# Attention decode with a gated feed-forward layer on one core: the first keys go ahead of the weights into the values' buffer, keys and values share one tensor, and the last values come in six loads instead of nine

## The chip, the core and the metric

The kernel runs on one core of a Trainium2 chip. The metric is the device time of one execution in microseconds, the median of several runs. A smaller time is better. The profile comes from one execution recorded by the hardware profiler.

## The reference

Two sequences (B = 2) of one token each go through one transformer block. All numbers are float32.

```
x: [2, 1, 448]; k_cache, v_cache: [2, 16, 8192, 256]; wq: [448, 4096]; wo: [4096, 448]
q      = layernorm(x) @ wq                     # 16 heads of 256, for each of 2 sequences
scores = q . k_cache * 256**-0.5               # 8192 keys a head
o      = softmax(scores) . v_cache
h      = x + o @ wo
g, u   = layernorm(h) @ w_gate, layernorm(h) @ w_up      # 448 -> 1792
out    = h + (g * u) @ w_down                  # 1792 -> 448
```

There are 32 pairs of a head and a sequence. The text calls each a query and numbers them 0 to 31. Each query has its own 8192 keys and 8192 values, 8.39 MB of either. Together with the weights this is 561 MB that have to come from the chip's memory.

## The kernel before

**Slots.** The 8192 keys of a query lie on 128 partitions, 64 keys on each. One key of all partitions is called a slot here: 256 floats on each of 128 partitions. "64 keys" or "32 values" in this document means so many slots. The buffer for keys, `k_sb`, has 112 slots (L245), the buffer for values, `v_sb`, has 64 (L246). Query i's keys go to the slots 0 to 63 for an even i and 48 to 111 for an odd i (L276). The 16 slots 48 to 63 thus belong to both, and the kernel works them off first (L446): for an even query they hold its last 16 keys, for an odd one its first 16.

**Work on a query.** VectorE multiplies the keys in place with the query (L462) and sums over the 256 numbers (L468), in two parts of 16 and 48 keys; the last two queries have four parts of 16 (L447). It then finds the maximum. TensorE and ScalarE make the softmax of it, and TensorE multiplies the weights of the softmax with the values (`mix`, L496). While VectorE works on query n, the values of query n-1 come in and are mixed. TensorE runs the mixes of the queries before `LOOP` in a hardware loop and the later ones in straight code.

**Loads.** Nearly all loads are issued by SyncE, on one queue, in the order of the program (L612 to L634): for each n the first part of the values of n-1, then the keys of n+1, then any further parts of the values of n-1, and every eighth query a block of weights. A helper (L146 to L176) finds out which earlier instructions still use the slots that a load writes, and puts waits for them ahead of the load. A waiting load holds up all loads behind it on SyncE. A wait for TensorE goes to the next of its matmuls that raises a semaphore; in a mix that is the last matmul of each part (L509).

**Query 0.** Its keys come in two loads, the last 24 of them and the first 40 (`FIRST`, L22), both behind the first block of weights (L303). The product of the 24 keys is written to the values' buffer (L459), so that the slots 48 to 63 are free for query 1's keys as soon as the multiply is over. The values of query 0 wait for that buffer.

**The end.** The values of the last four queries come in parts with places of their own (`LATE`, L25): 48 + 16 slots for query 28, 32 + 32 for 29, 32 + 32 for 30 (the second in the keys' buffer), 16 + 32 + 16 for 31. Behind them come the weights of the feed-forward layer (gate, up, down) into the keys' buffer (L660 to L670). After query 31's keys TensorE mixes its values, but ahead of the last part it starts the sums for the residual (`open_sums`, L598), then come the output projection of the last head, the gate and up projections, and the down projection, whose weights are the last to land.

Of the kernel before, what the change touches and what calls it, by code (L numbers as in the profile page):

```python
# [7 lines left out]
ALU = mybir.AluOpType  # L8
# [10 lines left out]
OVER = HC  # L19

AHEAD = 24
FIRST = ((NJ - AHEAD, NJ), (0, NJ - AHEAD))  # L22


LATE = (  # L25
    ((48, None), (16, None)),
    ((32, None), (32, None)),
    ((32, None), (32, ("k", 0))),
    ((16, ("k", 32)), (32, ("v", 32)), (16, ("v", 0))),
)  # L30
WQ, WO = 3 * 2 * DH + DH, 2 * D
WALL = 2 * WQ + 4 * WO
# [183 lines left out]
def decode_block(nc, x, k_cache, v_cache, w, wg, wu, wd, out):  # L216
# [3 lines left out]
    def sb(name, *shape):  # L220
        return nc.alloc_sbuf_tensor(name, list(shape), F32)[:]
# [20 lines left out]
        put("PE", "transpose", out, in_, ident[:n, :n], r=(*r, "ident"), w=w, mark=mark)  # L242

    sb("align", P, ALIGN)
    k_sb = sb("k_sb", P, 2 * NJ - OVER, DH)  # L245
    v_sb = sb("v_sb", P, NJ, DH)  # L246
    w_sb = sb("w_sb", P, WALL)
    buffers = {"k": k_sb, "v": v_sb}
    v_flat = v_sb.rearrange("p j d -> p (j d)")

    def guest(name, at, rows, *shape):

        n = 1
        for k in shape:
            n *= k
        o.homes[name] = ("v", at, n)
        got = v_flat[:rows, at : at + n]
        if len(shape) > 1:
            dims = "abc"[: len(shape)]
            got = got.rearrange(f"p ({' '.join(dims)}) -> p {' '.join(dims)}", **dict(zip(dims, shape)))  # L260
        return got
# [5 lines left out]
        h, b = divmod(i, B)  # L267
        return cache[b, h].rearrange("(p j) d -> p j d", p=P)[:, lo:hi, :]

    def load_keys(name, cache, i, lo, hi, buf, at, event=None):  # L270
        o.load(
            "SP", name, buffers[buf][:, at : at + hi - lo, :], keys(cache, i, lo, hi),
            writes=[(buf, at * DH, (at + hi - lo) * DH)], event=event,
        )

    def k_base(i):  # L276
        return i % 2 * (NJ - OVER)

    def load_k(i, lo=0, hi=NJ):
        load_keys(f"d_k_{i}_{lo}", k_cache, i, lo, hi, "k", k_base(i) + lo)  # L280

    def v_parts(i):
        got, lo = [], 0
        for n, place in LATE[i - EARLY] if i >= EARLY else ((NJ, None),):
            buf, at = place or ("v", lo)
            got.append((lo, lo + n, buf, at))
            lo += n
        return got

    def load_v(i, part):  # L290
        lo, hi, buf, at = part
        load_keys(f"d_v_{i}_{lo}", v_cache, i, lo, hi, buf, at, "e_v" if i < LOOP else None)

    def load_w(name, k, lo, hi, event=None):
        o.load("SP", name, w_sb[:, lo:hi], w[k][:, lo:hi], writes=[("w", lo, hi)], event=event)
# [4 lines left out]
    def wo_at(h):  # L300
        return 2 * WQ + h % 4 * WO

    load_w("d_w0", 0, 0, WQ)  # L303
    for lo, hi in FIRST:
        load_k(0, lo, hi)

    ident = sb("ident", P, P)
    put("POOL", "memset", ident, 0.0, w=["ident"])
# [134 lines left out]
    def score_parts(i):  # L443
        if i == 0:
            return list(FIRST)
        at = [(k - 1) % (NJ // HC) * HC if i % 2 == 0 else k * HC for k in range(NJ // HC)]  # L446
        if i in FINE:  # L447
            return [(lo, lo + HC) for lo in at]
        return [(at[0], at[0] + HC), (at[1], at[1] + NJ - HC)]

    def scores(i, part, between=None):
        h, b = divmod(i, B)
        s, name = s_t[i % 2], f"s{i % 2}"
        lo, hi = score_parts(i)[part]
        at = k_base(i) + lo
        kt = k_sb[:, at : at + hi - lo, :]
        qk, there = kt, ("k", at * DH, (at + hi - lo) * DH)
        if i == 0 and part == 0:
            qk, there = v_sb[:, : hi - lo, :], ("v", 0, (hi - lo) * DH)  # L459
        q, slot = qs[b], q_at(h)  # L460
        here = ("k", at * DH, (at + hi - lo) * DH)
        dve(  # L462
            "tensor_mul", qk, kt, q[:, slot, :][:, None, :].to_broadcast([P, hi - lo, DH]),
            r=[here, (f"q{b}", slot, slot + 1)], w=[there],
        )
        if between is not None:
            between()
        dve("tensor_reduce", s[:, lo:hi], qk, axis=AX.X, op=ALU.add, r=[there], w=[(name, lo, hi)])  # L468

    def top(i):  # L470
        dve("tensor_reduce", m, s_t[i % 2], axis=AX.X, op=ALU.max, r=[f"s{i % 2}"], w=["m"],
# [24 lines left out]
    def mix(i, parts):  # L496
        k = other(i)
        with common(i):
            take("e_v", i, 16)
            for lo, hi, buf, at in parts:  # L500
                for t in range(lo // 2, hi // 2):
                    g, j = 32 * (t % 4), at + 2 * t - lo
                    mm(
                        o_ps[k][g : g + 2, :], p_t[k][:, 2 * t : 2 * t + 2],
                        buffers[buf][:, j : j + 2, :], t < 4, t >= NJ // 2 - 4,
                        r=[f"p{k}", (buf, j * DH, (j + 2) * DH)], w=[f"o_ps{k}"],
                        mark="PE" if t == hi // 2 - 1 else None,
                    )

# [71 lines left out]
    def group(t, q):  # L581
        return t[:, q * YW : (q + 1) * YW]

    late_at = [HC * DH]

    def late_guest(name, rows, *shape):
        got = guest(name, late_at[0], rows, *shape)
        late_at[0] += o.homes[name][2]
        assert late_at[0] <= 2 * HC * DH
        return got  # L590

    h_sb = late_guest("h_sb", B, DC * P)
# [19 lines left out]
    for n in range(NQ + 1):  # L612
        hp, at = divmod(n, 2 * B)
        parts = v_parts(n - 1) if n > 0 else []
        if n > 0:
            load_v(n - 1, parts[0])
        if n < NQ:
            scores(n, 0, (lambda: softmax(n - 1)) if n > 0 else None)
        else:
            softmax(n - 1)  # L620
        if late is not None:
            mix(n - 2, late)
            mixed(n - 2)
            late = None
        if n + 1 < NQ:
            load_k(n + 1)
        for part in parts[1:]:
            load_v(n - 1, part)
        if n % 8 == 1:
            k = n // 8 + 1  # L630
            load_w(f"d_w_{k}", k, WQ if k == H // 4 else 0, WALL, event("e_w", n))
        def norm_last():
            if n > 0:
                norm(n - 1)  # L634

        if n == NQ:
            norm_last()
        else:
            for part in range(1, len(score_parts(n))):
                scores(n, part, norm_last if part == 1 else None)  # L640
        if n == NQ:
            mix(n - 1, parts[:-1])
            open_sums()
            mix(n - 1, parts[-1:])
            mixed(n - 1)
        elif n + 1 < NQ and len(parts) > 1:
            late = parts[1:]
            mix(n - 1, parts[:1])
        elif n > 0:
            mix(n - 1, parts)  # L650
            mixed(n - 1)
        if at == 2 and hp + 1 < H // 2:
            queries(n - 1, hp + 1)
        if n < NQ:
            if n == 0:
                o.ops["PE"].append(lambda: turns())
            top(n)

    k_flat = k_sb.rearrange("p j d -> p (j d)")
    places = {"wd": 0, "wg": (NJ - OVER) * DH, "wu": (NJ - OVER) * DH + NF * D}  # L660
    wd_t, wg_t, wu_t = (k_flat[:, places[n] :][:, : NF * D] for n in ("wd", "wg", "wu"))
    for name, t, src in (("wg", wg_t, wg), ("wu", wu_t, wu)):
        for k, half in enumerate(PIECES[name]):
            o.load("SP", f"d_{name}_{k}", t[:, half], src[:, half],
                   writes=[("k", places[name] + half.start, places[name] + half.stop)])
    at = 0
    for n in DOWN:
        o.load("SP", f"d_wd_{at}", wd_t[:, at * D : (at + n) * D], wd[:, at * D : (at + n) * D],
               writes=[("k", at * D, (at + n) * D)])
        at += n  # L670

    o.load(
# [6 lines left out]

    def project(out, out_name, t, name, k, between=None):  # L680
        wide, piece = WIDE[{"wg": "B_w_gate", "wu": "B_w_up"}[name]][k], PIECES[name][k]
        here = ("k", places[name] + piece.start, places[name] + piece.stop)
        t = t[:, piece]
        for c in range(DC):
            for g in range(4):
                xs = xr[:, c]
                if c < DC - 1:
                    at = c * sum(wide) + sum(wide[:g])
                else:
                    xs = xr[:, c + g % 2]  # L690
                    at = 3 * sum(wide) + (wide[0] if g >= 2 else 0)
                mm(
                    out[32 * g : 32 * g + 32, : wide[g]], xs.rearrange("p b r -> p (b r)"),
                    t[:, at : at + wide[g]], c == 0, c == DC - 1, r=["xr", here], w=[out_name],
                    mark="PE" if c == DC - 1 and g == 3 else None,
                )
            if c == 1 and between is not None:
                between()
# [54 lines left out]
    def down(lo, hi):  # L753
        for k in range(lo, hi):
            n, g = FF[k]
            for q in range(YN):
                mm(
                    y_ps[32 * q : 32 * q + 32, :], hmT[n // 2][:, n % 2, g, :],
                    wd_t[:, k * D + q * YW : k * D + (q + 1) * YW], False, k == NF - 1,
                    r=[f"hmT{n // 2}", ("k", k * D, (k + 1) * D)], w=["y_ps"],  # L760
                    mark="PE" if k == NF - 1 and q == YN - 1 else None,
                )

# [94 lines left out]
```

## Time and profile before

| | |
|---|---|
| median of 3 runs | 1301.37 us (1301.36 to 1301.38) |
| profiled execution, its span | 1300.5 us |
| rest of the median around the span | 0.9 us |
| VectorE busy | 1130.8 us (87%) |
| TensorE busy (matmul) | 488.8 us (38%) |
| ScalarE busy | 62.6 us (5%) |
| bytes moved, mean rate | 561.45 MB, 432 GB/s |

The span runs from the first to the last instruction of the profiled execution. Busy times are those of instructions that compute. Loads are issued by SyncE and carried out by 16 DMA engines. In the profile VectorE is DVE, TensorE is PE, ScalarE is ACT and SyncE is SP (its queue of issues SPq). Nearly all instructions have the line of a helper, L229 or L176, so that they are told apart by the tiles they write and read: `k_sb<-k_sb,q` is the multiply with the query, `s<-k_sb` the sum, `o_ps<-v_sb,p` the mix.

### The profile page before, as it was taken

The numbers are of one execution on the slowest core, as the hardware profiler recorded it, in microseconds if no ns is written. First come the engines' busy times: TensorE is split into PE (matmuls) and PEld (weight loads), VectorE is DVE, ScalarE is ACT, GpSimd is POOL, SyncE is SP. The second block draws the span as 40 slices with busy tenths as digits, with TensorE's granted clock in tenths as the row PEclk, the third lists the DMA queues.
The fourth block names the chain that finished last, engine by engine and source line by source line (L and its number), as shares of the span: only waits on it lengthen the run. The fifth ranks groups of instructions, "written<-read, shape, count | busy, mean of one in ns | idle before, by whom it ended". The sixth has DMA issues, their size and how long they took to land.

```text
span 1300.5 us, 6955 instructions
## 1 busy us (share of the span) xinstructions
PE 488.8 (38%) x2972; PEld 168.9 (13%) x2972; DVE 1130.8 (87%) x275; ACT 62.6 (5%) x184; POOL 1.4 (0%) x9
## 2 busy tenths in 40 slices
PE   3035422363331633215343063432424334243368
PEld 2011100120100201002101021010111001010113
DVE  7996988888988689888889868898888897889991
ACT  1000000000000000000000000000000000000000
POOL 0000000000000000000000000000000000000000
PEclk8566756686656766558666576665766667666578
DMA  9999999999999999999999999999999999999998
GB/s 414 423 434 448 424 437 431 427 441 423 448 424 435 448 423 443 427 439 429 435 435 423 433 448 423 448 424 443 427 443 427 423 436 445 426 438 429 435 433 374
DMA packets 12111, 561.45 MB, mean 432 GB/s; under 512 B 1602, under 2 KB 1732, under 8 KB 1988
## 3 DMA queue, kind: packets, MB, share of 16 engines
q1 hardware_dynamic: 12096, 561.30, 99.8%
q8 instruction: 6, 0.10, 0.0%
q14 instruction: 5, 0.04, 0.0%
q10 hardware_dynamic: 4, 0.00, 0.0%
HBM read 561.19 MB, written 0.11 MB: 432 GB/s over the span
## 4 chain that ended last, share of the span: by engine, by line
DMA 70%; DVE 29%; PE 0%; issue 0%; SPq 0%
DMA k_sb<-in_A_k_cache_dram 68%; DVE k_sb L229 14%; DVE s L229 14%; DMA k_sb<-in_wd_dram 2%; DVE nm L229 0%; PE y_ps L229 0%; SPq L176 0%; DVE m L229 0%; PE sm L229 0%; DVE v_sb L229 0%; DVE rl L229 0%
## 5 line engine op out<-in xcount | busy, mean ns | idle before, releaser
L229 DVE TENSOR_TENSOR k_sb<-k_sb,q 128x12288 f32<-128x12288 f32 (+2 forms) x67 | 549.6, 8203 | 130.3 <-DMA k_sb<-in_A_k_cache_dram 130.3
L229 DVE TENSOR_REDUCE s<-k_sb 128x48 f32<-128x12288 f32 (+2 forms) x67 | 549.3, 8198 | 0.2
L229 PE MATMUL o_ps<-v_sb,p 128*2 128x512 f32 x2000 | 288.2, 739 | 397.7 <-PEq L183 387.6
L229 PEld LDWEIGHTS o_ps<-v_sb,p 128*2 128x2 f32 x2000 | 53.7, 97 | 603.8 <-issue 591.3
L229 PE MATMUL sm<-nm,ones 1*128 1x1 f32 x64 | 16.6, 326 | 191.7 <-PEq L183 175.1
L229 PE MATMUL sm<-ident,m 128*1 128x128 f32 x32 | 10.9, 341 | 137.0 <-PEq L183 106.1
L229 PE MATMUL q_ps<-w_sb,xb 128*128 128x256 f32 (+1 forms) x172 | 59.3, 503 | 0.0
L229 ACT ACTIVATE o_sb<-o_ps 128x512 f32<-128x512 f32 x32 | 19.1, 597 | 703.9 <-PE o_ps L229 703.9
L229 PE MATMUL sm<-sel,o_sb 128*128 128x1 f32 x256 | 33.7, 253 | 25.8 <-PEq L183 22.9
L229 PE MATMUL acc_ps<-w_sb,oT 128*2 128x448 f32 x60 | 36.6, 749 | 15.9 <-PEq L183 11.0
L229 PEld LDWEIGHTS sm<-nm,ones 1*128 1x128 f32 x64 | 14.6, 283 | 201.2 <-issue 183.5
L229 PEld LDWEIGHTS sm<-sel,o_sb 128*128 128x128 f32 x256 | 31.8, 195 | 55.6 <-issue 48.2
L229 PEld LDWEIGHTS q_ps<-w_sb,xb 128*128 128x128 f32 x172 | 33.7, 200 | 30.0 <-issue 27.6
L229 PE MATMUL sm<-lsum,ones 128*128 128x1 f32 x64 | 17.5, 342 | 26.0 <-PEq L183 23.1
L229 ACT ACTIVATE nb<-sm 128x1 f32<-128x1 f32 x32 | 5.5, 171 | 395.7 <-PE sm L229 395.7
L229 PEld LDWEIGHTS sm<-ident,m 128*1 128x1 f32 x32 | 2.6, 81 | 149.8 <-issue 115.3
L229 PEld LDWEIGHTS sm<-lsum,ones 128*128 128x128 f32 x64 | 15.6, 303 | 28.0 <-issue 24.7
L229 ACT ACTIVATE q<-q_ps,rstd 128x512 f32<-128x512 f32 (+1 forms) x18 | 11.5, 640 | 71.9 <-PE q_ps L229 71.9
L229 PE MATMUL o_ps<-k_sb,p 128*2 128x512 f32 x48 | 9.3, 934 | 6.1 <-DMA k_sb<-in_A_v_cache_dram 6.1
L229 ACT ACTIVATE p<-s,nb 128x64 f32<-128x64 f32 x32 | 11.1, 347 | 1.0
L229 DVE TENSOR_TENSOR v_sb<-k_sb,q 128x6144 f32<-128x6144 f32 x1 | 6.6, 6557 | 4.8 <-DMA k_sb<-in_A_k_cache_dram 4.8
L229 PE MATMUL q_ps<-k_sb,xr 128*32 128x256 f32 (+3 forms) x96 | 10.0, 506 | 1.6 <-DMA k_sb<-in_B_w_gate_dram 1.6
(79 smaller groups left out, 85.1 us busy)
## 6 DMA issues: line engine op xcount, KB each, us to landing
v_sb<-in_A_v_cache_dram SPq DMA_DIRECT2D x4, 4096.0 KB, 30.5
w_sb<-in_w_dram SPq DMA_DIRECT2D x3, 3584.0 KB, 37.8
v_sb<-in_A_v_cache_dram SPq DMA_DIRECT2D x1, 6144.0 KB, 24.3
k_sb<-in_A_k_cache_dram SPq DMA_DIRECT2D x1, 5120.0 KB, 24.6
v_sb<-in_A_v_cache_dram SPq DMA_DIRECT2D x2, 2048.0 KB, 27.3
k_sb<-in_A_v_cache_dram SPq DMA_DIRECT2D x1, 4096.0 KB, 35.3
k_sb<-in_B_w_gate_dram SPq DMA_DIRECT2D x1, 3136.0 KB, 32.4
k_sb<-in_A_k_cache_dram SPq DMA_DIRECT2D x1, 3072.0 KB, 11.6
```

Source lines behind the costliest of these rows:

```text
L229: o.put(engine, lambda: f(*args, **kw), r, w, mark, event)
```

## The change

Keys and values share one tensor `c_sb` of 112 + 64 slots, whose last 64 (from `RING` on) are the values' buffer. Even queries now have the upper 64 of the 112 slots for keys and odd ones the lower 64. The 16 shared slots are still the first to be worked off: an even query's first 16 keys and an odd query's last 16.

Query 0's first 24 keys are loaded ahead of the weights, to the values' buffer, and multiplied in place there. Its other 40 keys follow behind the weights, to slots 72 to 111. Query 1's keys go to the slots 0 to 63, which nothing uses before.

The values of query 28 come in one load like those before it, so that TensorE's loop has 29 turns. Query 29 has 32 + 32 values, query 30 all 64 in one load to the slots 64 to 127 of the joint tensor, query 31 46 + 18, the 18 in slots 64 to 81. The weights of the feed-forward layer have other places in the slots, and the sums for the residual start ahead of the whole mix of query 31.

```diff
-FIRST = ((NJ - AHEAD, NJ), (0, NJ - AHEAD))
+FIRST = ((0, AHEAD), (AHEAD, NJ))
+RING = 2 * NJ - OVER
 LATE = (
-    ((48, None), (16, None)),
-    ((32, None), (32, None)),
-    ((32, None), (32, ("k", 0))),
-    ((16, ("k", 32)), (32, ("v", 32)), (16, ("v", 0))),
+    ((32, RING), (32, RING + 32)),
+    ((64, NJ),),
+    ((46, RING + 16), (18, NJ)),
 )
...
-    k_sb = sb("k_sb", P, 2 * NJ - OVER, DH)
-    v_sb = sb("v_sb", P, NJ, DH)
+    c_sb = sb("c_sb", P, RING + NJ, DH)
+    v_sb = c_sb[:, RING:, :]
...
     def k_base(i):
-        return i % 2 * (NJ - OVER)
+        return (1 - i % 2) * (NJ - OVER)
...
+    load_keys("d_k_first", k_cache, 0, *FIRST[0], RING)
     load_w("d_w0", 0, 0, WQ)
-    for lo, hi in FIRST:
-        load_k(0, lo, hi)
+    load_k(0, *FIRST[1])
...
-        at = [(k - 1) % (NJ // HC) * HC if i % 2 == 0 else k * HC for k in range(NJ // HC)]
+        at = [(k - i % 2) % (NJ // HC) * HC for k in range(NJ // HC)]
...
-        at = k_base(i) + lo
-        kt = k_sb[:, at : at + hi - lo, :]
-        qk, there = kt, ("k", at * DH, (at + hi - lo) * DH)
-        if i == 0 and part == 0:
-            qk, there = v_sb[:, : hi - lo, :], ("v", 0, (hi - lo) * DH)
+        at = RING if i == 0 and part == 0 else k_base(i) + lo
+        kt, here = c_sb[:, at : at + hi - lo, :], rows(at, hi - lo)
...
-    late_at = [HC * DH]
+    late_at = [0]
...
         if n == NQ:
-            mix(n - 1, parts[:-1])
             open_sums()
-            mix(n - 1, parts[-1:])
+            mix(n - 1, parts)
             mixed(n - 1)
...
-    places = {"wd": 0, "wg": (NJ - OVER) * DH, "wu": (NJ - OVER) * DH + NF * D}
+    places = {"wg": 0, "wu": NF * D, "wd": (NJ + 20) * DH}
```

## Rows read from the trace of the kernel before

**Rows 1.** The page: span, busy time of each engine, and the loads' queue.

```profile
span 1300.5 us, 6955 instructions
...
PE 488.8 (38%) x2972; PEld 168.9 (13%) x2972; DVE 1130.8 (87%) x275; ACT 62.6 (5%) x184; POOL 1.4 (0%) x9
...
q1 hardware_dynamic: 12096, 561.30, 99.8%
```

**Rows 2.** Windows: one query. Columns: busy PE, PEld, DVE, ACT, POOL; clock; DMA share; GB/s.

```profile
1120.77:1159.40 38.63, 14.69 (x81) 4.17 (x81) 35.01 (x7) 1.47 (x5) 0.00 (x0) 0.63 1.00 431
```

**Rows 3.** Chain of waits, queries 29 and 30: start us, length us, what.

```profile
1129.76 29.64 DMA k_sb<-in_A_k_cache_dram
...
1159.42 4.43 DVE k_sb L229
...
1164.03 4.33 DVE s L229
...
1194.47 4.33 DVE k_sb L229
...
1225.25 4.43 DVE s L229
```

**Rows 4.** Timeline of SyncE's issues, same stretch: start us, length us, what.

```profile
1168.39 0.33 SPq L176 DMA_DIRECT2D k_sb<-in_A_k_cache_dram  x1
1168.76 13.36 SPq L176 DMA_DIRECT2D v_sb<-in_A_v_cache_dram  x2
1203.34 0.33 SPq L176 DMA_DIRECT2D k_sb<-in_A_k_cache_dram  x1
```

**Rows 5.** Timeline of VectorE, query 0's first multiply; in brackets the idle time before.

```profile
12.83 6.56 DVE L229 TENSOR_TENSOR v_sb<-k_sb,q 128x6144 f32<-128x6144 f32 x1 [4.83 <-DMA k_sb<-in_A_k_cache_dram]
```

**Rows 6.** Timeline of TensorE, the first queries' matmuls.

```profile
7.30 9.25 PE L229 MATMUL q_ps<-w_sb,xb 128*128 128x256 f32 x32
```

**Rows 7.** Timeline of ScalarE, the first query scaled.

```profile
11.10 0.47 ACT L229 ACTIVATE q<-q_ps,rstd 128x256 f32<-128x256 f32 x1 [1.85 <-PE q_ps L229]
```

**Rows 8.** Chain of waits, query 2's keys from issue to landing.

```profile
57.05 27.09 DMA k_sb<-in_A_k_cache_dram
```

**Rows 9.** Timeline of TensorE, the first mix.

```profile
64.97 9.31 PE L229 MATMUL o_ps<-v_sb,p 128*2 128x512 f32 x64 [10.20 <-PEq L183]
```

**Rows 10.** DMA issues into an empty queue: count, KB, us from issue to landing.

```profile
w_sb<-in_w_dram SPq DMA_DIRECT2D x1, 896.0 KB, 4.8
...
out_dram<-v_sb SPq DMA_DIRECT2D x1, 56.0 KB, 1.6
```

**Rows 11.** Timeline of TensorE, mixes and matmuls that wait for loads at the end.

```profile
1207.80 6.20 PE L229 MATMUL o_ps<-v_sb,p 128*2 128x512 f32 x32 [0.75 <-DMA v_sb<-in_A_v_cache_dram]
...
1236.92 5.30 PE L229 MATMUL o_ps<-v_sb,p 128*2 128x512 f32 x32 [0.53 <-DMA v_sb<-in_A_v_cache_dram]
...
1256.26 5.87 PE L229 MATMUL o_ps<-k_sb,p 128*2 128x512 f32 x32 [6.05 <-DMA k_sb<-in_A_v_cache_dram]
...
1275.63 1.90 PE L229 MATMUL o_ps<-v_sb,p 128*2 128x512 f32 x16 [0.27 <-DMA v_sb<-in_A_v_cache_dram]
...
1283.13 3.63 PE L229 MATMUL q_ps<-k_sb,xr 128*32 128x512 f32 x16 [1.60 <-DMA k_sb<-in_B_w_gate_dram]
...
1296.47 2.03 PE L229 MATMUL y_ps<-k_sb,v_sb 128*32 128x112 f32 x64 [0.71 <-DMA k_sb<-in_wd_dram]
```

**Rows 12.** Timeline of TensorE, two whole mixes and one of 16 values.

```profile
1101.58 9.83 PE L229 MATMUL o_ps<-v_sb,p 128*2 128x512 f32 x64 [12.74 <-PEq L183]
...
1140.22 9.29 PE L229 MATMUL o_ps<-v_sb,p 128*2 128x512 f32 x64 [12.73 <-PEq L183]
...
1200.87 3.59 PE L229 MATMUL o_ps<-v_sb,p 128*2 128x512 f32 x16
```

**Rows 13.** Timeline of VectorE, the residual's copies.

```profile
1268.20 0.72 DVE L229 COPY v_sb<-acc_ps 2x448 f32<-2x448 f32 x2
```

More of the change, by code (lines that the diff above doesn't have):

```diff
@@ L244, in decode_block @@
     sb("align", P, ALIGN)
-    k_sb = sb("k_sb", P, 2 * NJ - OVER, DH)
-    v_sb = sb("v_sb", P, NJ, DH)
+    c_sb = sb("c_sb", P, RING + NJ, DH)
+    v_sb = c_sb[:, RING:, :]
     w_sb = sb("w_sb", P, WALL)
-    buffers = {"k": k_sb, "v": v_sb}
-    v_flat = v_sb.rearrange("p j d -> p (j d)")
+    c_flat = c_sb.rearrange("p j d -> p (j d)")
     def guest(name, at, rows, *shape):
@@ L255, in guest @@
             n *= k
-        o.homes[name] = ("v", at, n)
-        got = v_flat[:rows, at : at + n]
+        at += RING * DH
+        o.homes[name] = ("c", at, n)
+        got = c_flat[:rows, at : at + n]
         if len(shape) > 1:
@@ L268, in keys, with rows, load_keys @@
         return cache[b, h].rearrange("(p j) d -> p j d", p=P)[:, lo:hi, :]
-    def load_keys(name, cache, i, lo, hi, buf, at, event=None):
+    def rows(at, n):
+        return ("c", at * DH, (at + n) * DH)
+    def load_keys(name, cache, i, lo, hi, at, event=None):
         o.load(
-            "SP", name, buffers[buf][:, at : at + hi - lo, :], keys(cache, i, lo, hi),
-            writes=[(buf, at * DH, (at + hi - lo) * DH)], event=event,
+            "SP", name, c_sb[:, at : at + hi - lo, :], keys(cache, i, lo, hi),
+            writes=[rows(at, hi - lo)], event=event,
         )
     def k_base(i):
-        return i % 2 * (NJ - OVER)
+        return (1 - i % 2) * (NJ - OVER)
     def load_k(i, lo=0, hi=NJ):
-        load_keys(f"d_k_{i}_{lo}", k_cache, i, lo, hi, "k", k_base(i) + lo)
+        load_keys(f"d_k_{i}_{lo}", k_cache, i, lo, hi, k_base(i) + lo)
     def v_parts(i):
         got, lo = [], 0
-        for n, place in LATE[i - EARLY] if i >= EARLY else ((NJ, None),):
-            buf, at = place or ("v", lo)
-            got.append((lo, lo + n, buf, at))
+        for n, at in LATE[i - EARLY] if i >= EARLY else ((NJ, RING),):
+            got.append((lo, lo + n, at))
             lo += n
@@ L290, in load_v @@
     def load_v(i, part):
-        lo, hi, buf, at = part
-        load_keys(f"d_v_{i}_{lo}", v_cache, i, lo, hi, buf, at, "e_v" if i < LOOP else None)
+        lo, hi, at = part
+        load_keys(f"d_v_{i}_{lo}", v_cache, i, lo, hi, at, "e_v" if i < LOOP else None)
     def load_w(name, k, lo, hi, event=None):
@@ L454, in scores @@
         lo, hi = score_parts(i)[part]
-        at = k_base(i) + lo
-        kt = k_sb[:, at : at + hi - lo, :]
-        qk, there = kt, ("k", at * DH, (at + hi - lo) * DH)
-        if i == 0 and part == 0:
-            qk, there = v_sb[:, : hi - lo, :], ("v", 0, (hi - lo) * DH)
+        at = RING if i == 0 and part == 0 else k_base(i) + lo
+        kt, here = c_sb[:, at : at + hi - lo, :], rows(at, hi - lo)
         q, slot = qs[b], q_at(h)
-        here = ("k", at * DH, (at + hi - lo) * DH)
         dve(
-            "tensor_mul", qk, kt, q[:, slot, :][:, None, :].to_broadcast([P, hi - lo, DH]),
-            r=[here, (f"q{b}", slot, slot + 1)], w=[there],
+            "tensor_mul", kt, kt, q[:, slot, :][:, None, :].to_broadcast([P, hi - lo, DH]),
+            r=[here, (f"q{b}", slot, slot + 1)], w=[here],
         )
@@ L467, in scores @@
             between()
-        dve("tensor_reduce", s[:, lo:hi], qk, axis=AX.X, op=ALU.add, r=[there], w=[(name, lo, hi)])
+        dve("tensor_reduce", s[:, lo:hi], kt, axis=AX.X, op=ALU.add, r=[here], w=[(name, lo, hi)])
     def top(i):
@@ L499, in mix @@
             take("e_v", i, 16)
-            for lo, hi, buf, at in parts:
+            for lo, hi, at in parts:
                 for t in range(lo // 2, hi // 2):
@@ L504, in mix @@
                         o_ps[k][g : g + 2, :], p_t[k][:, 2 * t : 2 * t + 2],
-                        buffers[buf][:, j : j + 2, :], t < 4, t >= NJ // 2 - 4,
-                        r=[f"p{k}", (buf, j * DH, (j + 2) * DH)], w=[f"o_ps{k}"],
+                        c_sb[:, j : j + 2, :], t < 4, t >= NJ // 2 - 4,
+                        r=[f"p{k}", rows(j, 2)], w=[f"o_ps{k}"],
                         mark="PE" if t == hi // 2 - 1 else None,
@@ L588, in late_guest @@
         late_at[0] += o.homes[name][2]
-        assert late_at[0] <= 2 * HC * DH
+        assert late_at[0] <= HC * DH
         return got
@@ L657, in decode_block @@
             top(n)
-    k_flat = k_sb.rearrange("p j d -> p (j d)")
-    places = {"wd": 0, "wg": (NJ - OVER) * DH, "wu": (NJ - OVER) * DH + NF * D}
-    wd_t, wg_t, wu_t = (k_flat[:, places[n] :][:, : NF * D] for n in ("wd", "wg", "wu"))
+    places = {"wg": 0, "wu": NF * D, "wd": (NJ + 20) * DH}
+    wd_t, wg_t, wu_t = (c_flat[:, places[n] :][:, : NF * D] for n in ("wd", "wg", "wu"))
     for name, t, src in (("wg", wg_t, wg), ("wu", wu_t, wu)):
@@ L664, in decode_block @@
             o.load("SP", f"d_{name}_{k}", t[:, half], src[:, half],
-                   writes=[("k", places[name] + half.start, places[name] + half.stop)])
+                   writes=[("c", places[name] + half.start, places[name] + half.stop)])
     at = 0
@@ L668, in decode_block @@
         o.load("SP", f"d_wd_{at}", wd_t[:, at * D : (at + n) * D], wd[:, at * D : (at + n) * D],
-               writes=[("k", at * D, (at + n) * D)])
+               writes=[("c", places["wd"] + at * D, places["wd"] + (at + n) * D)])
         at += n
@@ L681, in project @@
         wide, piece = WIDE[{"wg": "B_w_gate", "wu": "B_w_up"}[name]][k], PIECES[name][k]
-        here = ("k", places[name] + piece.start, places[name] + piece.stop)
+        here = ("c", places[name] + piece.start, places[name] + piece.stop)
         t = t[:, piece]
@@ L759, in down @@
                     wd_t[:, k * D + q * YW : k * D + (q + 1) * YW], False, k == NF - 1,
-                    r=[f"hmT{n // 2}", ("k", k * D, (k + 1) * D)], w=["y_ps"],
+                    r=[f"hmT{n // 2}", ("c", places["wd"] + k * D, places["wd"] + (k + 1) * D)],
+                    w=["y_ps"],
                     mark="PE" if k == NF - 1 and q == YN - 1 else None,
```

## The prediction, made before the changed kernel ran

> **What bounds the kernel now.** I read the page's shares first: one DMA queue carries 561 MB and its packets fill 99.8% of the 16 DMA engines' span, while VectorE, the busiest engine, has 1130.8 of 1300.5 us [rows 1]. Then one query of the steady part: in 38.63 us the DMA share is 1.00 and VectorE works 35.01 us [rows 2]. So VectorE idles 3.6 us in each query, and the queue never does. The 38.63 us move one query's keys and values, 16.78 MB, at 434 B/ns: 19.32 us for 64 keys (or values), 0.302 us for one. Last the chain of waits [rows 3] beside the issues of SyncE's queue [rows 4]. Query 29's keys land at 1159.40 and VectorE starts on them 0.02 us later. Each load is issued well before the one ahead of it has landed, so the only way to lose time is to let the queue run empty, and the only way to gain it is to send fewer bytes, start earlier or finish sooner after the last byte. The change does none of the last three: the bytes, their sum in the first transfers and the work behind the last weights stay. The profiled span is 1300.5 us, 0.9 below the median of 1301.37; I add differences to the median.
>
> **The change part by part.**
>
> *The first transfers.* Query 0's first 24 keys go ahead of the weights, and query 1's keys, which had to wait for the first multiply, are issued at once behind query 0's rest. The two first loads together are as long as before, so the weights now land where the keys did, at about 12.8 us [rows 5]. From PE's first query matmul at 7.30 [rows 6] to the scaled query on ScalarE, 11.10 + 0.47 [rows 7], took 4.3 us; VectorE thus starts at about 17.1 instead of 12.8. It hands this on: query 2's keys, issued at 57.05 [rows 8], go out at 61.4. The load then running is query 0's values; TensorE takes them up at 64.97 [rows 9], so 3.6 us are still queued. What an issue into an empty queue costs is in [rows 10]: 896 KB landed 4.8 us after the issue and would need 2.1 at 434 B/ns, so 2.7 on top; 56 KB out landed after 1.6, 0.1 of it bytes, so 1.5 on top. As 3.6 is over 2.7, the queue stays full. Values 0 are issued 4 us later too, behind 19 us of query 1's keys. VectorE's delay dies in the next queries' idle 3.6 us. Cost 0; without the cover, what is missing of 2.7 us.
>
> *Slots swapped, one tensor, product in place.* Even queries now sit in the upper 64 of the 112 key slots and odd ones in the lower. The 16 shared slots are still read first, the multiplies have the same shapes, and each buffer is waited for as before. TensorE's loop takes 29 turns instead of 28, and its mixes take as long inside as outside. Cost 0 from query 1 to query 28.
>
> *Values 28 in one load instead of 48 + 16.* Here something moves. Before, the order in the queue was 48 values, query 30's keys, 16 values, 32 values of query 29, query 31's keys: issues at 1168.39 (keys 30), from 1168.76 (two loads of values) and 1203.34 (keys 31) [rows 4]. Query 30's keys so landed 16 values (4.83 us) earlier than the rhythm, and VectorE went from query 29 to query 30 without a wait, at 1194.47 [rows 3]. Now all 64 values are ahead of keys 30, which land at 1159.40 + 38.63 = 1198.03. VectorE waits 3.6 us, and all that follows on it is 3.6 us later. Query 31's keys need the shared slots, so SyncE waits for the first 16 keys' reduce: from landing to issue it took 1159.40 to 1168.39 = 8.99 us [rows 3, 4], so 1207.02. Behind keys 30 the queue holds only 32 values of query 29, 9.66 us, which land at 1207.69. The issue comes 0.67 us before the queue's last byte lands, where the same place had 4.4 us before (1203.34 against values taken up at 1207.80 [rows 11]). With a fixed part of 1.5 to 2.7 us [rows 10], keys 31 land at 1207.02 + 19.32 + 1.5 to 2.7 = 1227.8 to 1229.0; in a full queue 1227.0. The gap costs **0.8 to 2.0 us**. The 896 KB load is the nearer row in kind (a load over all engines), but it is also the program's first; I take the middle, **1.4**. Below, the cost could be nothing, if the fixed part is hidden to 0.7 us by the queue still draining. All bytes behind come later by this gap, and nothing gives it back, as the queue is full to the end.
>
> The Trainium skill, in "DMA: Bandwidth & Descriptors", section "Latency and other measured facts", gives about 0.6 us to the first byte for SyncE's loads. By that figure alone the issue at 1207.02 would be served just before 1207.69, and the sum would be without a gap; the trace's first load, 2.7 us above its bytes, speaks against so little.
>
> *The last loads, six for nine.* What a cut costs in a full queue: the second half of values 30 is taken up at 1256.26 and the last of values 31 at 1275.63, each with a wait for the load just ahead [rows 11]. Between them three loads of 64 values in all took 19.37 us, where one load takes 19.32. A cut is worth some 0.02 us, three **0.1 at most**.
>
> The Trainium skill says otherwise, in "DMA: Bandwidth & Descriptors", section "Anatomy of one DMA — SWDGE (gpsimd) path": each DMA pays about 2 us plus its bytes. By it three loads fewer would be an estimated 6 us faster; that page speaks of another issuing path, and the rows show the fixed part overlapped by the next load.
>
> *Covers of the new last loads.* The first 32 values of query 29 wait for the whole mix of values 28: landed at 1178.7, mixed at 1188.5 [rows 12], with the queue full to 1198. Values 30 (64 in one load) wait for query 30's last reduce: 1229.68 [rows 3] + 3.6 = 1233.3; queued are keys 31 and 32 values, to 1228.4 + 9.66 = 1238.1, so 4.8 us against at most 2.7. Values 31a (46) wait for the mix of values 29, 1238.1 + 5.3 [rows 11] = 1243.4; the queue lasts to 1257.4. Values 31b (18) wait for the whole mix of values 30, since TensorE marks only its last matmul: 1257.4 + 9.29 to 9.83 [rows 12] = 1267.2 at most; the queue lasts 46 x 0.302 = 13.9 us longer, to 1271.3. That leaves 4.1 against 2.7. All the weights stand behind this wait on SyncE, so it is the next to be late. The rest of the weights wait for query 31's reduces and that mix, all over by 1269, with over 10 us of bytes ahead.
>
> *The last stretch on TensorE.* VectorE's copies for the residual end at 1268.92 [rows 13] + 3.6 = 1272.5; the 16 small matmuls now stand ahead of the mix of values 31. The 46 values then take 5 us, the 18 another 1 to 1.9, to 1279.5 to 1280.4, where before plus 1.4 would be 1278.9. TensorE's wait for the gate weights was 1.60 us and for the last weights 0.71 [rows 11]; both move with the queue, so the 0.6 to 1.5 are hidden in the first. Uncovered, they cost up to 0.8.
>
> Sum: + 1.4 - 0.1 = + 1.3; 1301.37 + 1.3 = **1302.7 us**.
>
> **Rivals.** *Covered* (18 in 100): the engines still drain the 32 values when the new packets come, or the fixed part is small. Then only the saved cuts show: 1301.3, not slower. For it: 0.67 us are left at the issue. Against: [rows 10] show 1.5 at the least.
>
> *A second gap at values 31b* (8 in 100), the slower side: the granted clock stands at 0.63 in the mean of a query [rows 2], so between its levels of 1.2 and 2.4 GHz by turns, and 16 records alone took 3.59 us [rows 12]. At that pace the 64 records of 64 values take 14.4, the issue comes at 1271.8, and 1271.8 + 1.5 to 2.7 against 1271.3 is a gap of 2.0 to 3.2: 1302.7 + 2.6 = 1305.3. It decides from a mix of 11.2 to 12.4 us. Against: the whole mixes in the rows took 9.29 to 9.83 us.
>
> *A gap at the start* (6 in 100): the queries come over 1 us later than 17.1, because TensorE has been idle for 5 us, and keys 2 miss the end of values 0. Priced 1.0: 1303.7. Against: TensorE was nearly idle ahead of 7.30 as well, and the 4.3 us are from that state.
>
> *Fewer loads each save their fixed part* (1 in 100): 3 x 2.7 = 8.1, so 1293.3. The 19.37 us for three loads contradict it.
>
> **How the numbers follow.** A difference under 0.2%, 2.6 us, can't be told from none here. The forecast has 62 in 100, and 5 more are unnamed (3 of them slower by over 2.6 us, 1 faster). Faster by 0.2%: the last rival and the unnamed, 2 in 100. Slower by 0.2%: most of the second gap, a little of the start's, the unnamed, 11 in 100. The same: 87. The range for 8 in 10 goes from the covered case less some noise at the start, 1301.0, to the forecast's upper end with part of TensorE's stretch, 1304.0.
>
> **What would show it.** Right: VectorE waits about 3.6 us for keys 30, to 1198; keys 31 are issued near 1207 and land some 20.7 us later (1227.1 - 1203.3 = 23.8 before); the DMA share dips for 1 to 2 us behind 1207; the last weights land 1.3 us later. The first query's multiply starts near 17.1 with no dip at 62. Wrong: keys 31 issued before 1205, a dip elsewhere (near 62 or 1271), or an end that moves while the last weights' landing doesn't.

## The result and the profile after

The changed kernel takes 1306.72 us (median of 5 runs, 1305.23 to 1308.45), the one before 1301.36 in the same runs (1301.29 to 1301.38): a ratio of 1.0041, 95% interval 1.003 to 1.0052. It is slower by 5.4 us where 1.3 were forecast, and outside the range. The profiled execution is the slowest of the five, 1308.45 us with a span of 1307.1, 6.6 over that of before. The page of after, against [rows 1]: VectorE's work is the same to the digit, and the loads' queue carries the same bytes in fewer packets.

```profile
span 1307.1 us, 6967 instructions
...
PE 485.9 (37%) x2972; PEld 168.4 (13%) x2972; DVE 1130.8 (87%) x275; ACT 62.6 (5%) x184; POOL 1.4 (0%) x9
...
q1 hardware_dynamic: 11664, 561.30, 99.4%
```

Its share fell from 99.8% to 99.4%, 0.4% of 1307 or about 5 us in which the DMA engines stood still. To find where, I set the same windows beside each other: around query 2's keys, and around the issue of query 31's keys. Columns: busy PE, PEld, DVE, ACT, POOL; clock; DMA share; GB/s. Before:

```profile
62.00:66.00 4.00, 1.03 (x8) 0.29 (x12) 4.00 (x1) 0.00 (x0) 0.00 (x0) 0.50 1.17 508
1207.00:1212.00 5.00, 4.25 (x21) 0.70 (x24) 5.00 (x3) 0.26 (x1) 0.00 (x0) 0.50 1.03 446
```

After:

```profile
62.00:66.00 4.00, 1.15 (x8) 0.29 (x12) 4.00 (x1) 0.00 (x0) 0.00 (x0) 0.50 1.14 377
1207.00:1212.00 5.00, 2.05 (x12) 0.40 (x16) 5.00 (x2) 0.00 (x0) 0.00 (x0) 0.50 0.68 236
```

A window counts a packet whole where it starts, so that a share can pass 1 and the bytes say more. The second dip was forecast; the first, 131 GB/s for 4 us or some 1.2 us of bytes, was forecast not to be there. The steps in between are in VectorE's timeline (in brackets the idle time before): the first multiply, query 3's and query 30's. The first answers to [rows 5], the second to this row of before:

```profile
131.25 4.43 DVE L229 TENSOR_TENSOR k_sb<-k_sb,q 128x4096 f32<-128x4096 f32 x1 [12.04 <-DMA k_sb<-in_A_k_cache_dram]
```

After:

```profile
16.80 6.56 DVE L229 TENSOR_TENSOR c_sb<-c_sb,q 128x6144 f32<-128x6144 f32 x1 [8.81 <-ACT q L229]
...
133.25 4.43 DVE L229 TENSOR_TENSOR c_sb<-c_sb,q 128x4096 f32<-128x4096 f32 x1 [11.55 <-DMA c_sb<-in_A_k_cache_dram]
...
1200.27 4.42 DVE L229 TENSOR_TENSOR c_sb<-c_sb,q 128x4096 f32<-128x4096 f32 x1 [3.58 <-DMA c_sb<-in_A_k_cache_dram]
```

SyncE's issues, against 57.05 [rows 8] and 1203.34 [rows 4]:

```profile
60.67 0.33 SPq L176 DMA_DIRECT2D c_sb<-in_A_k_cache_dram  x1
...
1209.23 0.33 SPq L176 DMA_DIRECT2D c_sb<-in_A_k_cache_dram  x1
1209.61 60.49 SPq L176 DMA_DIRECT2D c_sb<-in_A_v_cache_dram  x4
```

And TensorE, against [rows 9] and [rows 11]:

```profile
64.85 9.94 PE L229 MATMUL o_ps<-c_sb,p 128*2 128x512 f32 x64 [6.45 <-PEq L183]
...
1209.95 5.69 PE L229 MATMUL o_ps<-c_sb,p 128*2 128x512 f32 x32 [3.12 <-DMA c_sb<-in_A_v_cache_dram]
...
1259.99 9.70 PE L229 MATMUL o_ps<-c_sb,p 128*2 128x512 f32 x64 [9.05 <-DMA c_sb<-in_A_v_cache_dram]
...
1288.91 3.31 PE L229 MATMUL q_ps<-c_sb,xr 128*32 128x512 f32 x16 [0.66 <-DVE xr L229]
...
1301.50 2.15 PE L229 MATMUL y_ps<-c_sb 128*32 128x112 f32 x64 [0.71 <-DMA c_sb<-in_wd_dram]
```

The 6.6 us of this execution, in order: query 3's keys come 2.0 later (133.25 against 131.25), and 0.2 more by query 30 (1200.27, against the 1198.03 forecast). Between the values taken up at 1209.95 and those at 1259.99 lie 64 keys and 96 values, 160 x 0.302 = 48.3 us of bytes (before, [rows 11]: 1236.92 + 19.34 = 1256.26); so 1209.95 + 48.3 = 1258.25, and the gap behind the issue at 1209.23 is 1.7. From the values of query 30 to the last weights it is 41.5 us instead of 40.2 (1296.47 - 1256.26): 1.3. The store of the output takes 3.1 us from issue to landing, 1.6 before: 1.5. Together 2.2 + 1.7 + 1.3 + 1.5 = 6.7. The median has 5.4.

### The profile page after: what moved, and what is told of

Its sections match the earlier page's. It is cut to its first block, busy times and chain, and to the rows that moved or that the text cites. A ratio compares the mean times of both kernels' runs of the same rounds, so it can differ in the third digit from the quotient of the medians.

```text
span 1307.1 us, 6967 instructions
## 1 busy us (share of the span) xinstructions
PE 485.9 (37%) x2972; PEld 168.4 (13%) x2972; DVE 1130.8 (87%) x275; ACT 62.6 (5%) x184; POOL 1.4 (0%) x9
## 3 DMA queue, kind: packets, MB, share of 16 engines
q1 hardware_dynamic: 11664, 561.30, 99.4%
## 4 chain that ended last, share of the span: by engine, by line
DMA 69%; DVE 30%; PE 0%; issue 0%; SPq 0%; ACT 0%
DMA c_sb<-in_A_k_cache_dram 66%; DVE c_sb L229 15%; DVE s L229 15%; DMA c_sb<-in_wd_dram 2%; DMA w_sb<-in_w_dram 1%; DVE nm L229 0%; PE q_ps L229 0%; PE y_ps L229 0%; SPq L176 0%; DVE m L229 0%; ACT q L229 0%; DVE rl L229 0%
## 5 line engine op out<-in xcount | busy, mean ns | idle before, releaser
L229 DVE TENSOR_TENSOR c_sb<-c_sb,q 128x4096 f32<-128x4096 f32 (+1 forms) x68 | 556.1, 8178 | 141.1 <-DMA c_sb<-in_A_k_cache_dram 132.3
L229 DVE TENSOR_REDUCE s<-c_sb 128x16 f32<-128x4096 f32 (+1 forms) x68 | 555.8, 8174 | 0.2
L229 PE MATMUL o_ps<-c_sb,p 128*2 128x512 f32 x2048 | 297.0, 744 | 407.5 <-PEq L183 395.3
L229 PEld LDWEIGHTS o_ps<-c_sb,p 128*2 128x2 f32 x2048 | 55.5, 97 | 621.9 <-issue 608.8
L229 ACT ACTIVATE oT<-sm,rl 128x2 f32<-128x2 f32 x32 | 8.4, 262 | 38.4 <-PE sm L229 38.4
L229 PE MATMUL q_ps<-c_sb,xr 128*32 128x256 f32 (+3 forms) x96 | 9.2, 472 | 0.7 <-DVE xr L229 0.7
```

The source lines that it names most:

```text
L229: o.put(engine, lambda: f(*args, **kw), r, w, mark, event)
```

## The experiments

Each is compared with the runs of the kernel before in its own batch (medians 1301.40, 1301.46 and 1301.46). The theory at first: the start costs something that I had put at nothing, and the single load of values 28 costs the rest through the gap. The rival: all 5.4 us come from the end.

**The two parts taken apart.** *Weights first*: the weights go ahead of query 0's 24 keys again.

```diff
-    load_keys("d_k_first", k_cache, 0, *FIRST[0], RING)
     load_w("d_w0", 0, 0, WQ)
+    load_keys("d_k_first", k_cache, 0, *FIRST[0], RING)
```

> The changed kernel with one part undone: the first block of weights goes ahead of the first 24 keys again; all else as changed. Theory (two gaps in the load queue: one near 62 us because the late weights make VectorE and so query 2's keys 3.6 us late, worth 2.0 us; one at query 31's keys, worth 1.8): the first gap goes, query 2's keys are issued near 57, query 3's keys land near 131.2, the gap at query 31's keys stays; about 1304.7 us. Rival A (all of the loss lies at the end, values 28 in one load): no change, 1306.7. Rival B (the joint tensor, the swapped slots or the product in place make every stage slower): no change, 1306.7, with no single step in the landings.

Measured: 1304.86 us (1304.34 to 1306.1), ratio 1.0027 [1.0018, 1.0037]. That is 1.86 under the changed kernel: the order of the first loads costs this much, as expected, and the rival that the end takes everything falls.

*Values 28 cut*: 48 + 16 again, with which TensorE's loop has 28 turns again; the rest as changed.

```diff
 LATE = (
+    ((48, RING), (16, RING + 48)),
     ((32, RING), (32, RING + 32)),
```

> The changed kernel with another part undone: query 28's values come as 48 + 16 again, so that query 30's keys have only 48 values ahead of them; all else as changed, weights behind the first keys. Theory of two gaps: query 31's keys are issued some 5 us before the queue's last load lands, the gap at 1207 to 1210 goes, the one near 62 stays; about 1304.9 us. Rival A (all of the loss at the end): about 1301.5. Rival B (layout): 1306.7.

Measured: 1303.41 us (1301.53 to 1305.1), 1.0017 [1.0008, 1.0026]; 3.31 under the changed kernel and 1.5 under the 1304.9 of the theory, between that and the rival. Its runs spread over 3.6 us, where the kernel before spreads over 0.7; the profiled one, the quickest, has no loss at the start at all (query 3's multiply at 131.07).

*Both undone*: the one tensor, the swapped slots and the product in place stay.

```diff
-    load_keys("d_k_first", k_cache, 0, *FIRST[0], RING)
     load_w("d_w0", 0, 0, WQ)
+    load_keys("d_k_first", k_cache, 0, *FIRST[0], RING)
...
 LATE = (
+    ((48, RING), (16, RING + 48)),
     ((32, RING), (32, RING + 32)),
```

> Both parts undone: weights ahead of the first keys, values 28 as 48 + 16; the joint tensor, the swapped slots, 64 values of query 30 in one load and 46 + 18 of query 31 stay. Theory of two gaps: 1301.2 to 1302.2 us (the last stretch, where the profile of the changed kernel lost another 1 us, decides within that range). Rival B (layout): stays near 1306.

Measured: 1301.59 us (1301.19 to 1302.66), 1.0003 [0.9994, 1.0012]: the layout costs nothing that shows. The parts add up: 1.82 for the start (second less third), 3.27 for values 28 (first less third), 5.1 of the 5.4.

**The start: how late is too late.** In the kernel before, a second sum over M of query 0's first 24 products keeps VectorE busy M x 0.27 us longer and changes nothing else.

```diff
         dve("tensor_reduce", s[:, lo:hi], qk, axis=AX.X, op=ALU.add, r=[there], w=[(name, lo, hi)])
+        if i == 0 and part == 0:
+            dve("tensor_reduce", s[:, lo:lo + M], qk[:, :M, :], axis=AX.X, op=ALU.add, r=[there],
+                w=[(name, lo, lo + M)])
```

M = 14, 3.8 us late:

> The kernel before with nothing of the change, but VectorE held up by 3.8 us: the sum over the first 14 of query 0's 24 products is done a second time, right behind the first. Theory (what costs 2.0 us at the start is the lateness of query 2's keys alone): they are issued near 60.7 instead of 57.05, and the time is 1303.4 us, about 2.0 over the kernel before. Rival C (the loss at the start comes from the place or order of the first keys and weights): 1301.4, no change. The prediction's own price, an issue 4 us ahead of the landing is early enough, says 1301.4 too.

M = 7, 1.9 us late:

> The kernel before with VectorE held up by 1.9 us (the sum over 7 of query 0's first products done twice). Query 2's keys are issued near 58.6, some 6 us ahead of the landing of query 0's values. Theory (a lead of 5.5 us or more costs nothing): 1301.4 us. Rival (the loss grows with the delay from the first): 1301.6 to 1302.

M = 20, 5.5 us late:

> The kernel before with VectorE held up by 5.5 us (20 products summed twice). Query 2's keys are issued near 62, 2.7 us ahead of the landing. Theory (below a lead of some 4 us the engines run empty): a gap at 62 to 66 us, plus later stalls of single engines that are no longer hidden; 1303.5 to 1304.5 us. The prediction's price (2.7 us of lead is enough) says 1301.4. Rival (the loss is noise of the engines and not of the lead): as with 3.8 us, 1302.

And the same with M = 14 in the third kernel above, which has the layout of after:

> Both parts undone as in the third experiment (1301.6 us), and VectorE held up by 3.8 us at the start through a second sum over 14 of query 0's first products, so that query 2's keys are issued near 60.6, as in the changed kernel, with the weights first. Theory (the cost of the start is the lateness of query 2's keys alone): 1303.4 us as the second experiment, which has the weights behind the keys and nothing else different. Rival (the order of the first loads costs by itself): 1302.0, as the lateness gave on the kernel before.

Measured, with the lead (take-up of query 0's values less the issue of query 2's keys):

```
kernel                issue    lead   median us (range)            over its base
before                57.05    7.9    1301.40 (1301.23 to 1301.88)   -
M = 7                 58.50    6.3    1301.47 (1301.23 to 1301.81)   0.0
M = 14                60.36    4.4    1301.96 (1301.62 to 1304.12)   0.6
M = 14, layout after  60.65    4.1    1303.06 (1301.27 to 1305.05)   1.5
values 28 cut         60.67    4.0    1303.41 (1301.53 to 1305.10)   1.8
M = 20                61.95    2.9    1302.93 (1302.51 to 1304.37)   1.5
```

A lead of 6.3 us is free; near 4 it costs 0.6 to 1.8, by the run between nothing and 3.5; at 2.9 it always costs. The theory's prices were too high: it had 1303.4 for M = 14 and 1303.5 to 1304.5 for M = 20. Lateness alone makes the loss on the layout of after, where the weights come first (1303.06 against 1303.41 with values 28 cut); why M = 14 costs less on the kernel before isn't shown, and the ranges overlap.

The loss is not all at the start. In the trace with M = 14 on the layout of after, query 3's multiply is only 0.75 late (131.67 against 130.92 in the kernel with both undone) and query 30's values 0.2, yet the last weights come 1.35 later:

```profile
1256.23 9.84 PE L230 MATMUL o_ps<-c_sb,p 128*2 128x512 f32 x64 [8.21 <-DMA c_sb<-in_A_v_cache_dram]
...
1297.67 2.05 PE L230 MATMUL y_ps<-c_sb 128*32 128x112 f32 x64 [0.68 <-DMA c_sb<-in_wd_dram]
```

The same two rows with both undone:

```profile
1256.02 8.69 PE L230 MATMUL o_ps<-c_sb,p 128*2 128x512 f32 x64 [8.13 <-DMA c_sb<-in_A_v_cache_dram]
...
1283.22 3.60 PE L230 MATMUL q_ps<-c_sb,xr 128*32 128x512 f32 x16 [0.66 <-DVE xr L230]
...
1296.32 1.98 PE L230 MATMUL y_ps<-c_sb 128*32 128x112 f32 x64 [0.72 <-DMA c_sb<-in_wd_dram]
```

The packet records show the reason, though no run isolates it. The 16 DMA engines don't finish a load together: the last packets of query 0's values end between 62.44 and 62.85 on fifteen engines and at 64.42 on one in the changed kernel, much as in the kernel before (62.56 to 63.15, and 64.37). So fifteen engines run dry up to 2 us before the landing that I had counted from. Seen from their ends, the lead of 4.2 us was 1.8 to 2.2 us (60.67 to 62.44 and 62.85), that of M = 7 was 3.9 to 4.4 (58.50 to 62.42 and 62.91) and that of M = 20 was 0.5 to 1.0 (61.95 to 62.43 and 62.92). In the changed kernel their first packets of query 2's keys then start between 62.59 and 64.22, and nine of the fifteen take 3.3 to 3.8 us instead of 2.42. In the trace with values 28 cut, issued at the same 60.67, nearly all start at once and take 2.42; what decides between the two isn't shown.

What an engine loses there is at first only its head start over the slowest. Late in the program 16 KB instruction fetches hold single engines for 0.9 us each (before: from 1233.81, 1268.88, 1286.71 and 1296.49). The packets of one engine follow each other without a pause, so those on either side of a fetch can be found. In the kernel before, the fetch of 1268.88 meets an engine that is ahead, and it ends the last 16 values at 1275.16, no later than the slowest (1275.21). With M = 14 on the layout of after, the fetch of 1272.36 meets an engine with no head start, which ends the last 18 values at 1276.51, where the next one ends at 1275.25.

**A cut in a full queue.** In the kernel before, the keys of queries 1 to 31 go in two loads each, the half that is worked on last ahead of the other.

```diff
-            load_k(n + 1)
+            cut = [(0, NJ // 2), (NJ // 2, NJ)]
+            for lo, hi in cut if (n + 1) % 2 == 0 else cut[::-1]:
+                load_k(n + 1, lo, hi)
```

> The kernel before with the keys of queries 1 to 31 each in two loads of 32 instead of one of 64, the half that is worked off first loaded last, so that VectorE starts when all have landed as before: 31 loads more. Theory (a load in a full queue costs only some 0.02 us): 31 x 0.02 = 0.6, about 1302.0 us. Rival (each load pays a fixed part of about 2 us, or the 1.5 to 2.7 us seen at an empty queue): over 1345 us.

Measured: 1302.76 us (1302.66 to 1302.9), 1.001 [1.0001, 1.0019]. Of 31 more loads each costs 1.30 / 31 = 0.042 us, twice what I had read from the trace; three fewer give back 0.13. The rival that each has a fixed part of its own of about 2 us is out by a factor of some fifty.

**The end: queue or TensorE.** *Values 29 as 48 + 16*, in the first kernel (weights first, values 28 whole), with query 30's values as 32 + 32: 48 values instead of 32 then stand in the queue when query 31's keys are issued, so it can't run dry, while VectorE stays 3.6 us late.

```diff
 LATE = (
-    ((32, RING), (32, RING + 32)),
-    ((64, NJ),),
+    ((48, RING), (16, RING + 48)),
+    ((32, NJ), (32, NJ + 32)),
     ((46, RING + 16), (18, NJ)),
```

> Weights ahead of the first keys as in the first experiment, values 28 whole as in the change, but query 29's values cut 48 + 16 instead of 32 + 32 (and query 30's 32 + 32, so that its first half need not wait for query 30's last sum). Query 30's keys still land a rhythm late, near 1198, and query 31's keys are still issued near 1207, but now 48 values are queued behind keys 30 instead of 32, so the issue comes 5.5 us ahead of the landing. Theory (what costs 3.3 us at the end is the queue run empty at query 31's keys): about 1301.5 us. Rival (the whole load of values 28, or the delay of VectorE by 3.6 us itself, costs it, through the last stretch on TensorE): about 1304.8, as the first experiment.

Measured: 1305.41 us (6 runs, 1303.03 to 1306.48), 1.003 [1.0017, 1.0042]. A miss: the theory that only the empty queue costs falls. The profiled run took 1303.37. In it keys 31 are issued at 1206.54 and the values ahead are taken up at 1212.11, a lead of 5.6, the queue loses nothing behind them (1212.11 + 144 x 0.302 = 1255.6, taken up at 1255.71), and the chain of waits from 1255 to the output's store has no transfer in it (start us, length us, what):

```profile
1263.91 4.43 DVE s L229
...
1273.17 9.15 PE o_ps L229 x64
...
1286.91 2.93 PE q_ps L229 x14
...
1292.95 2.59 PE q_ps L229 x42
...
1298.03 2.10 PE y_ps L229 x80
```

TensorE's last mix starts 3.0 us later than with both undone (1270.12 there) and takes 0.7 longer (9.17 for 64 records against 8.46), so the gate's matmuls come at 1286.91 instead of 1283.22, 3.7 late. With both undone the waits for the last weights took what is left over; here they vanish, and 1.8 us reach the end (1300.08 against 1298.30), as in the time of this run. The 2 us more in the other runs have no trace.

*Mix ahead of the sums*, in that kernel: the first part of the last mix goes ahead of the 16 small matmuls, as before the change.

```diff
         if n == NQ:
+            mix(n - 1, parts[:1])
             open_sums()
-            mix(n - 1, parts)
+            mix(n - 1, parts[1:])
```

> The kernel of the sixth experiment (weights first, values 28 whole, no gap in the queue, 1305.4 us) with one thing undone: TensorE mixes query 31's first 46 values ahead of the sums for the residual, not behind them, so it need not wait for VectorE's copies (0.9 us) and the 16 small matmuls (some 1 us) before it starts. New theory (there TensorE's last stretch sets the end): 1.5 to 2 us faster, about 1303.7. Old theory (the load queue sets the end): no change, 1305.4.

Measured: 1303.84 us (1303.22 to 1304.77), 1.0019 [1.0009, 1.0028]. The median is 1.57 lower, the ranges overlap, and in the two traces TensorE ends no earlier (1300.56 against 1300.08). So the order of sums and mix isn't shown to matter; what stays in both is VectorE's 3.6 us.

*The gap alone*: both parts undone, so VectorE is on time, and only query 31's keys wait for one thing more, query 29's norm, which comes 4 us later.

```diff
+        def more_loads(reads=()):
+            if n + 1 < NQ:
+                load_k(n + 1, reads=reads)
...
+                if n == NQ - 2 and part == 1:
+                    more_loads(["rl1"])
```

> Both parts undone as in the third experiment (1301.6 us), and one wait added: query 31's keys also wait for query 29's reciprocal, which VectorE does 4.3 us after the sum they wait for anyway. They are issued near 1207.5, just when the 32 values ahead of them have landed, as in the changed kernel, but VectorE and with it TensorE's last stretch are on time. New theory (the end of the changed kernel has two costs side by side: the empty queue, some 1.6 to 2.5 us, and TensorE's last stretch, 3.6 us late through VectorE): the gap alone gives 1303.2 to 1304. If the gap is worth nothing by itself: 1301.6. If it is all of the 3.3 us: 1305.

Measured: 1305.63 us (1305.39 to 1306.17), 1.0032 [1.002, 1.0044], 1.6 to 2.4 more than expected. The issue falls on the very end of the queue. First SyncE, then TensorE:

```profile
1207.47 0.33 SPq L177 DMA_DIRECT2D c_sb<-in_A_k_cache_dram  x1
```

```profile
1207.51 5.31 PE L230 MATMUL o_ps<-c_sb,p 128*2 128x512 f32 x32 [1.56 <-DMA c_sb<-in_A_v_cache_dram]
...
1259.29 8.64 PE L230 MATMUL o_ps<-c_sb,p 128*2 128x512 f32 x64 [8.12 <-DMA c_sb<-in_A_v_cache_dram]
...
1300.02 1.99 PE L230 MATMUL y_ps<-c_sb 128*32 128x112 f32 x64 [0.72 <-DMA c_sb<-in_wd_dram]
```

1207.51 + 48.3 = 1255.81, so 3.5 us are lost behind a lead of 0.04. By the packet records they are two losses. The last packets of query 29's first 32 values end at 1207.14 and those of query 31's keys at 1228.91, 21.77 us apart for 19.32 us of bytes: the gap is 2.5. It leaves the engines level (the keys end within 0.6 us of each other), and the fetch of 1233.25 then costs 0.9 in the next 32 values (1239.50 on its engine, 1238.59 on the next). With weights first the lead was 0.71 and the gap 1.9:

```profile
1207.41 6.15 PE L229 MATMUL o_ps<-c_sb,p 128*2 128x512 f32 x32 [3.11 <-DMA c_sb<-in_A_v_cache_dram]
...
1257.60 8.39 PE L229 MATMUL o_ps<-c_sb,p 128*2 128x512 f32 x64 [8.74 <-DMA c_sb<-in_A_v_cache_dram]
...
1272.93 9.25 PE L229 MATMUL o_ps<-c_sb,p 128*2 128x512 f32 x64
...
1287.65 3.59 PE L229 MATMUL q_ps<-c_sb,xr 128*32 128x512 f32 x16 [0.67 <-DVE xr L229]
...
1298.79 2.28 PE L229 MATMUL y_ps<-c_sb 128*32 128x112 f32 x80
```

Here TensorE no longer waits for the last weights, though the queue lost 1.9 us: the end is TensorE's. In the profiled run of the changed kernel, with the start's 2.2 us in the queue as well, it waits 0.71 for them again, and the end is the queue's. So the single load of values 28 makes two paths late at once, and their costs overlap instead of adding up to more than the 3.3 us: the gap alone cost 4.0 in the median, with 0.8 more of gap than the changed kernel had and the fetch on top, and VectorE's lateness alone 3.8 in the median and 1.8 in the traced run. How the 3.3 divide isn't shown.

No version of the change beats the kernel before; the nearest, with both undone, is the same.

## Why the prediction was wrong

*The first transfers: wrong.* The step that failed reads: as 3.6 us are still queued and that is over 2.7, "the queue stays full", "Cost 0". Its times were near: VectorE started at 16.80 (forecast 17.1), keys 2 were issued at 60.67 (61.4), and 4.2 us were still queued, more than I had counted on. The cost was 1.8. The fixed part of 2.7 had been read as landing less bytes of one load, and set against the landing of the load ahead, as if all 16 engines ended together. Fifteen of them ended 1.8 to 2.2 us behind the issue, less than the 2.7: 4.2 us of lead by the landing are not enough, 6.3 are. The rival of a gap at the start was nearer, but for its price (1.0) and its condition: it asked for queries later than 17.1, and they came earlier.

*Values 28 in one load: right in the wait and the gap.* VectorE waited 3.58 us (3.6). Less the 2.2 of the start, keys 31 were issued at 1207.0 (1207.02) with a lead of 0.72 (0.67). The gap was 1.7 in the changed kernel and 1.9 with weights first, in the 0.8 to 2.0 forecast and above the 1.4 taken. The fixed part, lead and gap together, was 2.5 and 2.6, and 2.5 with the queue just empty, inside the 1.5 to 2.7 taken. The 3.3 us of the load as a whole hold the next step too. The Trainium skill, "DMA: Bandwidth & Descriptors", section "Latency and other measured facts", speaks of a fixed cost of about 2 us per DMA and of 0.6 us to the first byte. The runs show 2.5 for the first; for the second, with the queue just empty, the first packet starts at 1208.42, 0.95 us after the issue of 1207.47 began and 0.62 after its 0.33 us were over, so that the trace agrees if it is counted from there.

*The last stretch on TensorE: wrong.* The step that failed: "the 0.6 to 1.5 are hidden in the first", with "up to 0.8" uncovered. I put the end of the last mix at 1279.5 to 1280.4. With weights first it is 1272.93 + 9.25 = 1282.2. The 46 + 18 records took 8.4 to 9.25 us where I had 6 to 6.9. The rows don't bear that sum out: [rows 12] have 9.29 to 9.83 for 64, and before the change the last query's three parts took 3.40 + 3.61 + 1.90 = 8.9 us together (the third is in [rows 11]):

```profile
1268.01 3.40 PE L229 MATMUL o_ps<-k_sb,p 128*2 128x512 f32 x16
1271.23 3.61 PE L229 MATMUL o_ps<-v_sb,p 128*2 128x512 f32 x32
```

So the mix hardly got slower; the forecast had priced all of it at the pace of its quick part. The granted clock goes with the pace. Before, it was 0.50, the level of 1.2 GHz, from 1268 to 1270, 0.73 from 1270 to 1272, and then 1.00, the level of 2.4 GHz, with more than half of the mix still to come:

```profile
1272.00:1276.00 4.00, 3.73 (x48) 0.92 (x44) 0.00 (x0) 0.00 (x0) 0.00 (x0) 1.00 1.07 457
```

With values 29 as 48 + 16 the mix starts at 1273.10, and it too has 0.50 at first:

```profile
1272.00:1276.00 4.00, 3.81 (x32) 1.03 (x36) 0.54 (x5) 0.00 (x0) 0.00 (x0) 0.50 1.03 442
```

From the end of its work on query 30 to the last query's maximum TensorE idled 1.54 us before and 5.25 us here. With weights first it idled only 1.03 us there and the mix took the longest, 9.25, so that this idle time alone doesn't decide. The gate's matmuls so started 4.4 us late with weights first (1287.65 against 1283.22), and 2.8 reached the end (1298.79 + 2.28 against 1296.32 + 1.98). I had priced the two paths as one behind the other, the later weights covering a later TensorE; as both came late, there was no cover.

*Behind values 30: left out.* 1.3 us between the values of query 30 and the last weights of the changed kernel, as in two runs with a late start alone (41.4 and 41.6 us for 40.2), and not in three others. By the records an instruction fetch falls in that stretch in all of them. In the changed kernel it runs from 1264.47 to 1265.34 between two packets of query 31's first 46 values, and its engine ends this load at 1274.57, where the other fifteen end between 1273.20 and 1273.63: 0.9 of the 1.3. In the two runs with a late start the engine with the fetch is the last of its load as well, by 1.3 us (1276.51, the next 1275.25) and 1.9 us (1272.07, the next 1270.22); with both undone it ends beside the next (1274.95 and 1274.90) and costs nothing that shows. So by these traces the fetch is most of it. The store of 3.1 us stays open: a fetch of 1.15 us begins at 1304.84 beside it, in one traced execution.

*The rest: right.* Swapped slots, one tensor and the product in place cost nothing that shows. No second gap came at the last 18 values: they were issued at 1269.77, 3.4 us and more ahead of the engines' ends (1273.20 at the earliest), and on the middle engine they end 5.65 us behind the load ahead, for 5.4 us of bytes. Cuts cost 0.042 us each instead of 0.02, too little to show. The Trainium skill's 2 us per DMA ("DMA: Bandwidth & Descriptors", section "Anatomy of one DMA — SWDGE (gpsimd) path") are not added by a load in a full queue: 31 loads more cost 1.30 us together.

## What to carry to other kernels

Where one queue bounds a kernel, measure every issue by its lead over the landing of the load ahead, and don't count a lead as safe because it exceeds the fixed part read from one load: the engines end at different times, here up to 2 us apart, and it is their own ends that the lead has to be counted to. The loss can show only a thousand microseconds later, when something holds an engine that has no head start left. When an edit makes an engine late, follow it on every path to the end, and ask of each cover whether the same edit moves it too. Don't price a long stretch of matmuls by the pace of its quickest part. Splitting a load in a full queue is cheap, so a cut that brings the next keys forward is worth more than the fewest loads.

## What the runs showed of the hardware

- A load issued 0.04 to 0.7 us before its queue runs out leaves a gap of 2.5 to 1.7 us, lead and gap together 2.5 to 2.6; at 4 us ahead of the landing the loss varies from run to run between nothing and 3.5 us; at 6.3 us there is none.
- The 16 engines end one load up to 2 us apart (62.44 to 64.42); behind a gap in the queue they end within 0.5 to 0.7 us of each other.
- One load more in a full queue costs 0.042 us (31 of them 1.30).
- Instruction fetches of 16 KB, five or six in each traced execution, hold one DMA engine each for 0.88 to 1.15 us. The queue loses that time where the engine has no head start (0.9 us in two kernels), and nothing where it has one.
- Sixty-four records of the same mix took 8.4 to 9.9 us in these traces, with the granted clock between its levels.
